# Stage 1 of a three-stage attention kernel: one hand-written issue sequence per pair of heads instead of a loop over tiles

## The chip, the cores and the metric

One core of one Trainium2 chip runs the whole program. The metric is the device time of one execution in microseconds (us): the median of several runs, set beside one execution that the hardware profiler recorded.

## What is computed

Three blocks run one after the other. Block 1, the one that the change touches, is attention whose queries are the means of two neighbouring positions, for 4 batches and 8 heads, with 576 queries, 1152 keys and head size 64:

```python
q_pool = q.reshape(B, H, S // 2, 2, D).mean(axis=3)
scores = scale * np.matmul(q_pool, k.transpose(0, 1, 3, 2))
scores = scores - np.max(scores, axis=-1, keepdims=True)
attn = np.exp(scores)
attn = attn / (np.sum(attn, axis=-1, keepdims=True) + 1e-09)
return np.matmul(attn, v).astype(np.float32)
```

Block 2 takes the result as 4 x 576 x 512 and runs causal attention with four experts, of which a gate picks two for each token. Block 3 multiplies a value projection by the sigmoid of a short causal convolution and projects the product.

## The kernel before

The program is scheduled by hand: each engine runs its instructions in the order in which the Python code issues them. It has three stages, one for each block. The change is in stage 1, lines 308 to 636.

**Tiles of stage 1.** The 8 heads of a batch go by twos, so there are 16 pairs (b, hp). The 576 queries of a head are four tiles of 128 rows and one of 64; the two rests of a pair share a tile. A pair thus has nine tiles, in two units (`UNITS`, line 390): unit 0 has the first two query tiles of both heads (tiles 0 to 3 of the pair), unit 1 the other two of both heads and the shared one (tiles 4 to 8). There are M = 144 tiles.

**What a tile goes through.** `scores` (line 394) multiplies a query tile by the keys, in three thirds g = 0, 1, 2 of 384 keys each. A third is two matmuls (L405), four for the shared tile; queries and keys are held as a high and a low part, which are added in PSUM. The tile's scores lie in three PSUM banks of pool `ps_s`, which has two such buffers. `rowmin` (L410, VectorE) takes the minimum of a row of all 1152 scores (they carry a minus sign). `expo` (L416, ScalarE) writes the exponentials to SBUF (tile `p`, three buffers) and their sums. `transp` (line 445) transposes a third on TensorE, three 128 x 128 transpositions (L453) into one bank of pool `ps_t`, which has two; one copy moves them from there into the unit's tile `pt`. For g = 0 and 1 the copy is on ScalarE (L461), for g = 2 on VectorE (L463).

**End of a unit.** `shares` (line 418) computes one over each row's sum on VectorE (L425, L426) and has GpSimd spread it (L431, L433). `av` (line 465) transposes these (L442, two or three matmuls; both banks used are of `ps_t`), has ScalarE copy them (L475, L479), and multiplies `pt` by the values, 18 pairs of matmuls (L483): the attention run. VectorE then multiplies by the shares (L485, tile `xf`), GpSimd splits the result, and a DMA writes it for stage 2. In the middle of `av`, `between` issues one `expo` and some steps of the preparation of later weights on VectorE (lines 92 to 105).

**What sets the order.** One loop over m (line 556) issues, in each turn, the transpositions of tile m - 2, the scores of tile m + 1, `expo(m)`, `shares(m - 1)` and pieces of other work: the queries and keys of the next pair on GpSimd (`prep`, L384, L361, L362, four pieces), which go to their place by DMA, the loads of the pair after that, and weight preparation. The thirds take turns in this order, in which 0 is a transposition and 1 a score group; after an attention run they alternate:

```python
for what, g in ((0, 0), (1, 0), (0, 1), (1, 1), (0, 2), (1, 2)) if burst else ((0, 0), (0, 1), (1, 0), (0, 2), (1, 1), (1, 2)):
```

Work that one turn produces for GpSimd or for DMA waits in the list `late` and is issued at the start of the next turn. After the last score tile, pieces of stage 2 (`fill`: projections L237 and L268) are issued between the transpositions.

Of the kernel before, what the change touches and what calls it, by code (L numbers as in the profile page):

```python
# [20 lines left out]
def tile_kernel(ctx, tc, q, k, v, w_gate, wq, wk, wv, wo, w_val, conv_w, w_out, wo_t, out):  # L21
    nc = tc.nc
    B, H, S, D = v.shape
# [20 lines left out]
                       fill=1.0, base=0, channel_multiplier=1)  # L44
# [8 lines left out]
                       fill=1e9, base=0, channel_multiplier=1)  # L53
# [162 lines left out]
    late2, urgent, rides = [], [], []  # L216
# [86 lines left out]

    G = 3
    GW = 3 * P

    s2 = ctx.enter_context(ExitStack())
    with ExitStack() as s1:
# [26 lines left out]
        pairs = [(b, hp) for b in range(B) for hp in range(H // 2)]  # L335
# [14 lines left out]
        def prep(n):  # L350
# [36 lines left out]

            return [lambda: one(0), qgroup, lambda: one(1), lambda: one(2)]

        UNITS = ([(0, 0), (0, 1), (1, 0), (1, 1)], [(0, 2), (0, 3), (1, 2), (1, 3), (2, 4)])  # L390
        tiles = [(n, u, i, ht) for n in range(len(pairs)) for u in range(2) for i, ht in enumerate(UNITS[u])]
        soft, pts, rss = {}, {}, {}
# [14 lines left out]
        def rowmin(m):  # L407
            d = soft[m]
            d["nm"] = st_p.tile([P, 1], F32, name="nm")
            dve.tensor_reduce(d["nm"], d["s"][:, :, 0:GW], axis=AX.XY, op=ALU.min)  # L410

        def expo(m):
            d = soft[m]
            n, u, i, _ = tiles[m]
            d["p"] = p_p.tile([P, G, GW], F32, name="p")
            act.activation(d["p"], d["s"][:, :, 0:GW], AF.Exp, bias=d["nm"], scale=-1.0, accum_out=sums[(2 * n + u) % len(sums)][:, i:i + 1])  # L416
# [28 lines left out]
        def transp(m, g):  # L445
            n, u, i, (h, t) = tiles[m]
            p = soft[m]["p"]
            if i == 0 and g == 0:
                pts[n, u] = pt_p.tile([P, C, 2, 256 + R64 * u], F32, name=f"pt{u}")
            pt = pts[n, u]  # L450
            ps = ps_t.tile([P, 512], F32, name="t")
            for j in range(3):
                pe.transpose(ps[:, j * P:(j + 1) * P], p[:, g, j * P:(j + 1) * P], ident)  # L453
            if h < 2:
                dst = pt[:, 3 * g:3 * g + 3, h, (t % 2) * P:(t % 2) * P + P]
                src = ps[:, 0:GW].rearrange("p (c k) -> p c k", k=P)
            else:
                dst = pt[:, 3 * g:3 * g + 3, :, 256:]
                src = ps[:, 0:GW].rearrange("p (c h k) -> p c h k", h=2, k=R64)
            if g < 2:  # L460
                act.activation(dst, src, AF.Copy)  # L461
            else:
                dve.tensor_copy(dst, src)  # L463
# [31 lines left out]
            late.append(high)  # L495

        Q0 = 2 * P
        PM = 1

        def first():  # L500

# [48 lines left out]
        load(1)  # L550
        nc.sync.dma_start(data[0][2], v[0, 0:2].rearrange("h (p c) d -> p h c d", p=P))
        bg, bgw = iter(()), iter(())
        LAG = 2
        M = len(tiles)
        burst, done = False, set()
        for m in range(-1, M + LAG + 4):
            if m == M - 9:
                assert not preps and next(bg, bg) is bg and next(bgw, bgw) is bgw
                s1a.close()
# [28 lines left out]
            now, late[:] = late[:], []  # L588
            for a in now:
                a()  # L590
            for what, g in ((0, 0), (1, 0), (0, 1), (1, 1), (0, 2), (1, 2)) if burst else ((0, 0), (0, 1), (1, 0), (0, 2), (1, 1), (1, 2)):
                if what == 0:
                    if 0 <= m - LAG < M:
                        transp(m - LAG, g)
                    if m >= M:
                        now2, late2[:] = late2[:], []
                        if fill:
                            fill.pop(0)[1]()
                        for a in now2:
                            a()  # L600
                        if urgent:
                            urgent.pop(0)()
                        if not fill and late2:
                            for a in late2:
                                a()
                            late2.clear()
                    if g == 1:
                        if m in (0, 1):
                            begin[m]()
                        if 0 <= m < M and m not in done:  # L610
                            expo(m)
                        if m in (2, 3):
                            begin[m]()
                    if g == 2:
                        if 0 <= m - 1 < M:
                            shares(m - 1)
                        if preps:
                            preps.pop(0)()
                elif 0 <= m + 1 < M:
                    scores(m + 1, g)  # L620
            if 0 <= m + 1 < M:
                rowmin(m + 1)
            burst = 0 <= m - LAG < M and tiles[m - LAG][2] == len(UNITS[tiles[m - LAG][1]]) - 1
            if burst:
                def between():
                    if m + 1 < M:
                        expo(m + 1)
                        done.add(m + 1)
                    for _ in range(9):
                        if next(bg, None):  # L630
                            break

                av(*tiles[m - LAG][0:2], between)
            next(bgw, None)
        for a in late:
            a()

# [452 lines left out]
```

## Time and profile before

| | |
|---|---|
| median of 3 runs | 794.48 us (794.35 to 795.16) |
| the profiled execution | 794.37 us |
| its span, first to last instruction | 792.6 us |
| mean granted clock of TensorE | 0.995 |
| busy in the span: TensorE, VectorE, ScalarE, GpSimd | 765.4, 541.9, 477.1, 304.7 us |
| transpositions of stage 1 (L453) | 1296, 278 ns of one |
| score matmuls (L405) | 960, about 370 ns of one |
| reductions (L410) | 144, 1348 ns of one |
| exponentials (L416) | 144, 1222 ns of one |
| copies on ScalarE (L461) | 288, 489 ns of one |
| copies on VectorE (L463) | 144, 558 ns of one |

How to read it. The span is what the profiler saw; the execution's own time is 1.8 us longer. The time of one instruction on TensorE runs from its start to a modelled end, and instructions overlap: the next starts before the one ahead has ended. So the sum of durations is more than the time that a sequence takes. Weight loads of TensorE have rows of their own (PEld). A share of busy time is a mean over three stages with different work; the rows below are therefore taken from stretches of stage 1, which ends with the last attention run.

### The profile page before, as it was taken

How to read it: one execution, taken by the hardware profiler on the slowest of the kernel's cores; microseconds unless marked ns; L12 is line 12 of the kernel's file. 1: busy time of each engine (PE TensorE's matmuls, PEld its weight loads, DVE VectorE, ACT ScalarE, POOL GpSimd, SP SyncE). 2: the span in 40 equal slices, each digit the busy share in tenths (PEclk: the TensorE clock that was granted, in tenths of full speed). 3: DMA queues.
4: the chain of work that ended last, by engine and by line, in shares of the span. 5: the costliest groups of instructions: out<-in, count | busy, mean ns of one | idle time of the engine just before them, and what ended most of it. 6: DMA issues, size and time to landing. Idle time of an engine off the chain costs nothing.

```text
span 792.6 us, 14790 instructions
## 1 busy us (share of the span) xinstructions
PE 765.4 (97%) x5332; PEld 625.5 (79%) x5332; DVE 541.9 (68%) x999; ACT 477.1 (60%) x1052; POOL 304.7 (38%) x412
## 2 busy tenths in 40 slices
PE   6899999999999999999999999997999999989998
PEld 4777877778778778778777787897988989877887
DVE  5666788778778878656655664355679898887730
ACT  5676677567667666766775675433464555648532
POOL 4454665664665665643433511021222222230000
PEclk9999999999999999999999999998999999999999
DMA  7777867868878688567458481455375454900112
GB/s 236 194 188 220 243 174 222 236 183 239 207 225 247 188 244 259 152 199 216 120 174 233 102 263 71 104 142 155 74 218 127 98 178 118 288 10 15 70 64 93
DMA packets 86248, 134.50 MB, mean 170 GB/s; under 512 B 21536, under 2 KB 58912, under 8 KB 86176
## 3 DMA queue, kind: packets, MB, share of 16 engines
q1 hardware_dynamic: 86176, 133.57, 59.6%
q8 instruction: 42, 0.69, 0.3%
q14 instruction: 30, 0.25, 0.1%
HBM read 53.37 MB, written 21.76 MB: 95 GB/s over the span
## 4 chain that ended last, share of the span: by engine, by line
PE 79%; DVE 10%; ACT 5%; DMA 2%; issue 2%; SPq 1%; POOLq 0%; ACTq 0%; DVEq 0%
PE s L405 19%; PE t L483 18%; PE t L453 15%; PE a L237 7%; PE o L1006 6%; PE a L268 4%; DVE nm L410 3%; ACT p L416 3%; PE a L798 3%; PE s L698 2%; PE a L663 2%; DVE gp L210 2%; DVE pt L463 1%; PE a L770 1%; PE t L442 1%
## 5 line engine op out<-in xcount | busy, mean ns | idle before, releaser
L410 DVE TENSOR_REDUCE nm<-s 128x1 f32<-128x1152 f32 x144 | 194.1, 1348 | 23.9 <-PE s L405 17.7
L461 ACT ACTIVATE pt<-t 128x384 f32<-128x384 f32 x288 | 132.6, 489 | 125.9 <-PE t L453 122.5
L453 PE MATMUL t<-ident,p 128*128 128x128 f32 x1296 | 204.8, 278 | 1.5 <-DVE pt L463 1.3
L416 ACT ACTIVATE p<-s,nm 128x1152 f32<-128x1152 f32 x144 | 176.0, 1222 | 36.8 <-DVE nm L410 34.1
L453 PEld LDWEIGHTS t<-ident,p 128*128 128x128 f32 x1296 | 150.9, 141 | 41.9 <-issue 13.5
L483 PE MATMUL t<-pt,vn 128*64 128x320 f32 (+1 forms) x1152 | 146.7, 408 | 0.1
L405 PE MATMUL s<-ka,qst 128*128 128x384 f32 x480 | 128.8, 372 | 8.6 <-ACT ka L535 6.8
L405 PE MATMUL s<-kb,qst 128*128 128x384 f32 x480 | 132.7, 369 | 1.4 <-ACT p L416 1.1
L483 PEld LDWEIGHTS t<-pt,vn 128*64 128x64 f32 x1152 | 80.0, 137 | 56.1 <-issue 5.0
L463 DVE COPY pt<-t 128x384 f32<-128x384 f32 x144 | 80.3, 558 | 63.9 <-PE t L453 59.3
L405 PEld LDWEIGHTS s<-ka,qst 128*128 128x128 f32 x480 | 77.9, 193 | 16.7 <-ACT p L416 8.9
L734 POOL TENSOR_TENSOR p<-p,sm 128x512 f32<-128x512 f32 (+3 forms) x32 | 40.1, 1253 | 114.3 <-DVE sm L732 85.9
L405 PEld LDWEIGHTS s<-kb,qst 128*128 128x128 f32 x480 | 77.6, 191 | 5.0 <-ACT p L416 1.7
L237 PE MATMUL a<-xh,wqk 128*128 128x288 f32 x384 | 59.6, 307 | 2.1 <-DVE pt L748 2.1
L485 DVE TENSOR_TENSOR xf<-t,rb 128x256 f32<-128x256 f32 (+1 forms) x32 | 14.7, 458 | 65.8 <-PE t L483 65.0
L237 PEld LDWEIGHTS a<-xh,wqk 128*128 128x128 f32 x384 | 54.7, 195 | 3.5 <-DVE pt L748 2.5
L431 POOL COPY rm<-rs 128x256 f32<-128x256 f32 x31 | 12.4, 398 | 92.2 <-PE t L453 58.5
L719 ACT ACTIVATE p<-s,nm 128x256 f32<-128x256 f32 (+3 forms) x64 | 33.0, 523 | 22.8 <-DVE nm L708 22.8
L362 POOL TENSOR_TENSOR hlk<-kt,hlk 128x384 fp32r<-128x384 f32 x45 | 45.5, 1010 | 1.1
L210 DVE SCALAR_TENSOR_TENSOR gp<-x,cw,gp 128x572 f32<-128x572 f32 (+3 forms) x48 | 41.0, 856 | 2.6 <-ACT gp L819 2.1
L492 POOL CAST xt<-xf 128x256 fp32r<-128x256 f32 (+1 forms) x32 | 13.6, 424 | 74.6 <-DVE xf L485 74.6
L708 DVE TENSOR_REDUCE nm<-s 128x2 f32<-128x512 f32 (+4 forms) x40 | 32.4, 811 | 1.4
(168 smaller groups left out, 1058.3 us busy)
## 6 DMA issues: line engine op xcount, KB each, us to landing
ka<-hlk SPq DMA_DIRECT2D x90, 192.0 KB, 3.2
kb<-hlk SPq DMA_DIRECT2D x90, 192.0 KB, 3.7
vn<-in_v_dram SPq DMA_DIRECT2D x16, 576.0 KB, 7.4
xh<-x_d SPq DMA_DIRECT2D x16, 576.0 KB, 6.5
k<-hl SPq DMA_DIRECT2D x32, 288.0 KB, 4.9
qt<-in_q_dram SPq DMA_DIRECT2D x15, 576.0 KB, 5.2
kt<-in_k_dram SPq DMA_DIRECT2D x15, 576.0 KB, 6.3
x_d<-xt SPq DMA_DIRECT2D x16, 320.0 KB, 4.0
```

The lines of the kernel that those rows point to most:

```text
L210: dve.scalar_tensor_tensor(out=gp[:, n:], in0=x[:, 0:SQ - n], scalar=cw[:, m, c:c + 1], in1=gp[:, n:], op0=ALU.mult, op1=ALU.add)
L237: pe.matmul(ps[:, 0:HQ], lhsT=wqk[wi][:, t, cs], rhs=xh[:, t, xi, qsl], start=o == 0, stop=o == len(ops) - 1)
L362: late.append(lambda: pool.tensor_tensor(out=hlk[:, 1, gs], in0=kt[:, gs], in1=f(hlk[:, 0, gs]), op=ALU.subtract))
L405: pe.matmul(ps[:, 0:GW], lhsT=a, rhs=c, start=o == 0, stop=o == len(ops) - 1)
L410: dve.tensor_reduce(d["nm"], d["s"][:, :, 0:GW], axis=AX.XY, op=ALU.min)
L416: act.activation(d["p"], d["s"][:, :, 0:GW], AF.Exp, bias=d["nm"], scale=-1.0, accum_out=sums[(2 * n + u) % len(sums)][:, i:i + 1])
L453: pe.transpose(ps[:, j * P:(j + 1) * P], p[:, g, j * P:(j + 1) * P], ident)
L461: act.activation(dst, src, AF.Copy)
L463: dve.tensor_copy(dst, src)
L483: pe.matmul(ps[64 * h:64 * h + 64, 0:N], lhsT=vn[:, h, j, :], rhs=pt[:, j, h, :], start=j == 0, stop=j == C - 1)
L734: pool.tensor_tensor(out=pv, in0=pv, in1=sm[:, :, None].to_broadcast([P, 2, w]), op=ALU.mult)
L1006: pe.matmul(ps[:, 0:w], lhsT=hl[xi][:, kt, t * P - a:(t + 1) * P - a], rhs=end3["wo3"][:, kt, wi, c:c + w], start=o == 0, stop=o == len(op ...
```

## The change

The loop over m is replaced by a string of 65 letters, issued once for each pair. T is one third of transpositions with its copy, S one score group, X an `expo`, H the `shares` of a unit, A the attention run of a unit (with an `expo` inside). Three tiles of scores are issued ahead. A second table, `EVAC`, says for each tile of a pair and each third whether its copy runs on ScalarE (A) or VectorE (D): 14 and 13 a pair, where it was 18 and 9. What a loop turn did besides (preparation, loads, the list `late`, the opening of stage 2's pools) is in `head(m)`, called ahead of the first score group of a tile; `filler` issues one piece of `fill`.

```diff
+        ORDER = "TSTSSTTXSTTSSHTTXSTTSSTTXSSSASTSSTXSTTSSTTXSTTSSHTTXSTTSSTTSTXSSA"
+        EVAC = ('DDA', 'ADD', 'AAD', 'DAA', 'DAD', 'DAA', 'DDA', 'ADD', 'AAA')
...
-            if g < 2:
+            if EVAC[m % 9][g] == "A":
                 act.activation(dst, src, AF.Copy)
             else:
                 dve.tensor_copy(dst, src)
...
-        for m in range(-1, M + LAG + 4):
+        def head(m):
...
+            if m >= M + 2:
+                for g in range(3):
+                    filler()
...
+        def score(k, g):
+            if g == 0:
+                head(k - 1)
+            if k < M:
+                scores(k, g)
+                if g == 2:
+                    rowmin(k)
+            if g == 2:
+                if preps:
+                    preps.pop(0)()
+                next(bgw, None)
+
+        def burst(m):
+            def between():
+                if m + 3 < M:
+                    expo(m + 3)
+                for _ in range(9):
+                    if next(bg, None):
+                        break
+
+            av(*tiles[m][0:2], between)
...
+        for n in range(len(pairs)):
+            for c in ORDER:
+                if c == "S":
+                    score(ns // 3, ns % 3)
+                    ns += 1
+                elif c == "T":
+                    transp(nt // 3, nt % 3)
+                    nt += 1
+                    if ns > 3 * M + 3:
+                        filler()
...
+                elif c == "X":
+                    if nx < M:
+                        expo(nx)
...
+                    nx += 1
+                elif c == "H":
+                    shares(9 * n + (3 if nt < 27 * n + 12 else 8))
+                elif c == "A":
+                    burst(nt // 3 - 1)
+                    nx += 1
```

The lines that follow show the order of instructions; in the changed kernel every line number of this part is higher by 4 (L405 is L409, L453 is L457, L463 is L467).

TensorE, unit 0 of a pair, from the attention run before it. `t<-ident,p` are transpositions, `s<-ka` and `s<-kb` scores of the two heads. Before:

```order
L483 MATMUL t<-pt_424,vn 64x320 x18
L453 MATMUL t<-ident,p 128x128 x3
L405 MATMUL s<-kb,qst_139 128x384 x2
L453 MATMUL t<-ident,p 128x128 x3
L405 MATMUL s<-kb,qst_139 128x384 x2
L453 MATMUL t<-ident,p 128x128 x3
L405 MATMUL s<-kb,qst_139 128x384 x2
L453 MATMUL t<-ident,p 128x128 x6
L405 MATMUL s<-ka,qst_138 128x384 x2
L453 MATMUL t<-ident,p 128x128 x3
L405 MATMUL s<-ka,qst_138 128x384 x4
L453 MATMUL t<-ident,p 128x128 x6
```

and with the change:

```order
L487 MATMUL t<-pt_427,vn 64x320 x18
L457 MATMUL t<-ident,p 128x128 x3
L409 MATMUL s<-kb,qst_139 128x384 x2
L457 MATMUL t<-ident,p 128x128 x3
L409 MATMUL s<-kb,qst_139 128x384 x4
L457 MATMUL t<-ident,p 128x128 x6
L409 MATMUL s<-ka,qst_138 128x384 x2
L457 MATMUL t<-ident,p 128x128 x6
L409 MATMUL s<-ka,qst_138 128x384 x4
L457 MATMUL t<-ident,p 128x128 x6
L409 MATMUL s<-ka,qst_138 128x384 x2
L457 MATMUL t<-ident,p 128x128 x6
```

Transpositions now come by sixes with two or four score matmuls between them; before, a three stood between the two score matmuls and the four.

VectorE in the same place. `xf` is the end of the attention run, `pt<-t` a copy, `nm<-s` a reduction, `rs` the shares. Before:

```order
L485 TENSOR_TENSOR xf_2560<-t,rb 128x320
L463 COPY pt_2618<-t 128x3x128
L410 TENSOR_REDUCE nm<-s 128x1
L463 COPY pt_2618<-t 128x3x128
L410 TENSOR_REDUCE nm<-s 128x1
L463 COPY pt_2618<-t 128x3x128
L425 TENSOR_SCALAR rs<-sums_142 128x4
L426 RECIPROCAL rs<-rs 128x4
L410 TENSOR_REDUCE nm<-s 128x1
```

and with the change:

```order
L489 TENSOR_TENSOR xf_2561<-t,rb 128x320
L467 COPY pt_2609<-t 128x3x128 x2
L414 TENSOR_REDUCE nm<-s 128x1
L467 COPY pt_2609<-t 128x3x128 x2
L414 TENSOR_REDUCE nm<-s 128x1
L429 TENSOR_SCALAR rs<-sums_142 128x4
L430 RECIPROCAL rs<-rs 128x4
L467 COPY pt_2609<-t 128x3x128 x2
L414 TENSOR_REDUCE nm<-s 128x1 x2
```

Copies come by twos ahead of each reduction, and the two small operations of the shares stand behind a reduction and ahead of two copies.

TensorE in the last pair, behind its last score group. The projections of stage 2 (`a<-xh`) follow. Before:

```order
L405 MATMUL s<-kb,qst_139 128x384 x2
L453 MATMUL t<-ident,p 128x128 x12
L237 MATMUL a<-xh,wqk_91 128x288
```

and with the change:

```order
L409 MATMUL s<-kb,qst_139 128x384 x2
L457 MATMUL t<-ident,p 128x128 x21
L237 MATMUL a<-xh,wqk_91 128x288
```

Seven thirds now stand in a row there instead of four.

## Rows read from the trace of the kernel before

**Rows 1.** Busy time by stretch: length, engines (instructions), granted clock, DMA share, GB/s.

```profile
core 0: us, PE busy (x) PEld busy (x) DVE busy (x) ACT busy (x) POOL busy (x), PEclk, DMA share, GB/s
...
160.00:220.00 60.00, 59.78 (x430) 46.33 (x428) 47.74 (x75) 39.96 (x79) 36.38 (x55) 1.00 0.77 213
...
498.00:501.00 3.00, 2.75 (x21) 2.41 (x20) 1.92 (x2) 2.01 (x5) 0.00 (x0) 1.00 0.00 0
...
542.50:549.50 7.00, 6.22 (x26) 5.86 (x26) 2.18 (x4) 1.52 (x6) 0.57 (x1) 0.52 0.33 129
```

**Rows 2.** Timeline, TensorE, unit 0 of a pair: start, length, engine, line, operation.

```profile
264.44 0.55 PE L453 MATMUL t<-ident,p 128*128 128x128 f32 x3
...
265.17 0.55 PE L453 MATMUL t<-ident,p 128*128 128x128 f32 x3
...
266.59 1.01 PE L453 MATMUL t<-ident,p 128*128 128x128 f32 x6
...
267.05 0.31 PEld L453 LDWEIGHTS t<-ident,p 128*128 128x128 f32 x3 [0.21 <-DVE pt L463]
...
267.35 0.60 PE L405 MATMUL s<-ka,qst 128*128 128x384 f32 x2
...
268.82 0.82 PE L453 MATMUL t<-ident,p 128*128 128x128 f32 x6
...
269.72 0.30 PEld L405 LDWEIGHTS s<-ka,qst 128*128 128x128 f32 x2 [0.32 <-ACT p L416]
...
273.37 0.38 PE L442 MATMUL t<-ident,rm 128*128 128x128 f32 x2
```

**Rows 3.** Timeline, TensorE, unit 1 of the same pair.

```profile
277.72 0.55 PE L453 MATMUL t<-ident,p 128*128 128x128 f32 x3
278.02 0.59 PE L405 MATMUL s<-kb,qst 128*128 128x384 f32 x2
278.45 0.49 PE L453 MATMUL t<-ident,p 128*128 128x128 f32 x3
278.69 0.59 PE L405 MATMUL s<-kb,qst 128*128 128x384 f32 x2
...
281.59 0.60 PE L405 MATMUL s<-ka,qst 128*128 128x384 f32 x2
...
283.07 0.82 PE L453 MATMUL t<-ident,p 128*128 128x128 f32 x6
283.64 0.59 PE L405 MATMUL s<-ka,qst 128*128 128x384 f32 x2
...
284.44 0.96 PE L405 MATMUL s<-ka,qst 128*128 128x384 f32 x4
...
289.74 0.49 PE L442 MATMUL t<-ident,rm 128*128 128x128 f32 x3
```

**Rows 4.** Timeline, VectorE (DVE) and ScalarE (ACT), unit 0 of that pair.

```profile
265.75 0.49 ACT L461 ACTIVATE pt<-t 128x384 f32<-128x384 f32 x1 [0.24 <-PE t L453]
...
266.44 0.56 DVE L463 COPY pt<-t 128x384 f32<-128x384 f32 x1 [1.32 <-PE t L453]
...
266.91 1.35 DVE L410 TENSOR_REDUCE nm<-s 128x1 f32<-128x1152 f32 x1
...
268.35 1.22 ACT L416 ACTIVATE p<-s,nm 128x1152 f32<-128x1152 f32 x1 [0.23 <-DVE nm L410]
...
269.02 1.36 DVE L410 TENSOR_REDUCE nm<-s 128x1 f32<-128x1152 f32 x1
...
269.57 0.86 ACT L461 ACTIVATE pt<-t 128x384 f32<-128x384 f32 x2
...
271.18 0.19 DVE L425 TENSOR_SCALAR rs<-sums 128x4 f32<-128x4 f32 x1
...
271.50 1.33 DVE L410 TENSOR_REDUCE nm<-s 128x1 f32<-128x1152 f32 x1
```

**Rows 5.** Timeline, TensorE, last pair: from its last score group to stage 2's first projection.

```profile
498.65 0.82 PE L453 MATMUL t<-ident,p 128*128 128x128 f32 x6
...
500.40 0.78 PE L237 MATMUL a<-xh,wqk 128*128 128x288 f32 x4
```

More of the change, by code (lines that the diff above doesn't have):

```diff
@@ L305, in tile_kernel @@
     GW = 3 * P
+    xh_p = y12_p = xh = wv3 = hl2 = c2 = qs = ks = v_p = g_p = ps_m = v2s = gws = None
+    fill = []
     s2 = ctx.enter_context(ExitStack())
@@ L497, in tile_kernel @@
         Q0 = 2 * P
-        PM = 1
         def first():
@@ L552, in tile_kernel @@
         bg, bgw = iter(()), iter(())
-        LAG = 2
         M = len(tiles)
-        burst, done = False, set()
-        for m in range(-1, M + LAG + 4):
+        def head(m):
+            nonlocal preps, bg, bgw
+            nonlocal xh_p, y12_p, xh, wv3, hl2, c2, qs, ks, v_p, g_p, ps_m, v2s, gws, fill
             if m == M - 9:
@@ L590, in tile_kernel @@
                 a()
[L591 to L634, printed above, removed]
+            if m >= M + 2:
+                for g in range(3):
+                    filler()
@@ new lines, in filler @@
+        def filler():
+            now2, late2[:] = late2[:], []
+            if fill:
+                fill.pop(0)[1]()
+            for a in now2:
+                a()
+            if urgent:
+                urgent.pop(0)()
+            if not fill and late2:
+                for a in late2:
+                    a()
+                late2.clear()
+        def score(k, g):
[9 more added lines that the diff above has]
+                next(bgw, None)
@@ new lines, in burst @@
+        def burst(m):
[6 more added lines that the diff above has]
+            av(*tiles[m][0:2], between)
+        ns, nt, nx = 0, 0, 0
+        for m in range(3):
+            if m:
+                head(m - 1)
+                begin[m - 1]()
+                expo(m - 1)
+            else:
+                head(-1)
+            for g in range(G):
+                scores(m, g)
+            rowmin(m)
+            if m and preps:
+                preps.pop(0)()
@@ new lines, in tile_kernel @@
+        ns, nx = 9, 2
+        for n in range(len(pairs)):
[8 more added lines that the diff above has]
+                        filler()
+                    if nt == 2:
+                        expo(2)
+                        begin[2]()
+                        nx = 3
+                elif c == "X":
+                    if nx < M:
+                        expo(nx)
+                    if nx == 3:
+                        begin[3]()
+                    nx += 1
[4 more added lines that the diff above has]
+                    nx += 1
@@ L635, in tile_kernel @@
+        for m in range(M + 2, M + 7):
+            head(m)
         for a in late:
```

## The prediction

> **What bounds the kernel now.** I began with the busy time by stretch [rows 1]. Inside stage 1 TensorE is busy 59.78 of 60 us at a granted clock of 1.00; VectorE has 47.74 us, ScalarE 39.96. So only TensorE's own stream can be shortened. But "busy" hides waits here, since the end of a matmul is modelled: what counts is when the next group starts. So I went on to the timeline of TensorE through the two units of one pair [rows 2, 3], read from the start of one row to the start of the next, and to the timeline of VectorE and ScalarE beside it [rows 4].
>
> Call three transpositions (one PSUM bank, one copy) a T, and the two score matmuls of one third of a tile an S; S3.1 is third 1 of tile 3. Where nothing waits, a T that is followed by an S takes 0.24 us (278.45 to 278.69), a run of two T 0.57 (283.07 to 283.64), one S 0.43 (278.02 to 278.45), eight score matmuls 1.48 (281.59 to 283.07) [rows 3]. So one more T costs 0.33, one more S (1.48 - 0.43) / 3 = 0.35, two S 0.78.
>
> Unit 0 lasts from 264.44 to 273.37, 8.93 us [rows 2]. Its 12 T and 12 S at the undisturbed prices (six single T, three double, six single S, three double) make 6 x 0.24 + 3 x 0.57 + 6 x 0.43 + 3 x 0.78 = 8.07, so 0.86 us are waits. Unit 1 lasts from 277.72 to 289.74, 12.02 us [rows 3]; seven single T, four double, six single S, four double and the 1.48 make 11.14: 0.88 us of waits. That is 1.74 us a pair, 28 us in 16 pairs: all that any new order of the same matmuls can win.
>
> Two waits make most of it. **The bank of a T.** There are two PSUM banks for transpositions, so a T waits for the copy of the T two before it. The double T at 266.59 took 0.76 instead of 0.57 for that reason: the bank came free when VectorE's copy (266.44, 0.56 us) ended, and the weight load followed 0.05 us later [rows 2, 4]. **The score tile.** Scores have two buffers, so the first S of tile k+2 waits for the exponential of tile k: from the last S of a tile (ends 268.82) 0.20 us until the reduction starts (269.02) [rows 2, 4]; the reduction is 1.35, then 0.09 (266.91 to 268.35), the exponential 1.22, and 0.15 until the weight load at 269.72, which the profile puts down to it [rows 2, 4]. Sum: 0.20 + 1.44 + 1.22 + 0.15 = 3.01 us. Between these two points the old order has TT S T SS TT, 0.57 + 0.43 + 0.24 + 0.78 + 0.57 = 2.59: 0.42 us short, and the double T at 268.82 shows most of it, 0.90 instead of 0.57 [rows 2]. A restarted T loses 0.06 more (after the attention run the T at 277.72 takes 0.30, not 0.24 [rows 3]), so 0.05 + 0.06 = 0.11 lie between the end of a copy and an undisturbed stream.
>
> **The change, part by part.**
>
> *Order of TensorE.* Nothing is added or taken away; in mid-unit a tile becomes TT S TT SS. Between the last S of tile k and the first of k+2 there is now TT S TT SS TT, 0.57 + 0.43 + 0.57 + 0.78 + 0.57 = 2.92 us, plus the bank wait worked out next, 0.18: 3.10 against 3.01. The score wait goes, with 0.09 us to spare. What is late next is the bank. In TT S TT the third T comes 2 x 0.33 + 0.35 = 1.01 after the first, but its bank needs 0.53 (a T's start to its copy: 265.17 to 265.75 less the 0.06 of a restart) + 0.49 (that copy; two in a row take 0.86) + 0.11 = 1.13 [rows 2, 4]: a wait of 0.12. The old order shows just this where a double T starts undisturbed: the S and T that follow it last from 283.64 to 284.44, 0.80 instead of 0.43 + 0.24 [rows 3]. The fourth T needs the second copy on the same engine: 0.53 + 0.86 + 0.11 = 1.50 against 1.13 + 0.33 = 1.46, 0.05 more. So one such passage costs 0.18, and each unit has two of them (both with the first pair of copies on ScalarE): 0.36.
>
> *The rest of unit 0.* TensorE's restart after the long run of attention times V, 0.06 (the rows of the T at 264.44 and at 265.17 show 0.55, not 0.49), and as much for the second T, which waits for the bank of that run; both as now [rows 2]. The two small divisions (H in the table of letters) now sit ahead of two copies on VectorE: 0.32 us (271.18 to 271.50 [rows 4]), which makes T3.2 about 0.05 late. Sum 0.53 against 0.86: 0.33 won.
>
> *Unit 1.* It now begins with scores instead of a T. No row shows that entry; I keep the 0.06, between 0 and 0.15. Two passages 0.36; T8.1 behind copies that the divisions delayed, 0.05; T8.2 one S after T8.1, its bank at 1.13 against 0.33 + 0.33 + 0.05 + 0.35, 0.07. Sum 0.54 against 0.88: 0.34 won.
>
> *Copies.* Four a pair move from ScalarE to VectorE (13 and 14 instead of 9 and 18). In the fullest stretch a pair of 30.7 us holds 47.74 / 60 x 30.7 = 24.4 us of VectorE; 4 x 0.56 = 2.2 more make 26.7 of 30.0, 89%. On the path this costs nothing as long as a tile's round on VectorE is shorter than TensorE's 4 x 0.33 + 3 x 0.35 = 2.37 (2.55 with its bank wait). By the rows, where the next instruction starts 0.47 after a copy's start (266.44 to 266.91) [rows 4], the round is 0.47 + 0.47 + 1.35 = 2.29: it fits, and with the divisions, 2.61, it is late once by the 0.05 counted above. Without that overlap it would not fit (second rival).
>
> *What else moves.* The spreading of the shares stands before the next pair's query addition on GpSimd, not behind; its two copies have over 2 us before the attention run needs them, so nothing is gained or lost. The issues on SyncE keep their order but for two weight loads that trade places with a neighbour; no row of stage 1 has TensorE waiting for them. The key transfers keep their distance of five tiles.
>
> *The ends.* The first 27 us wait for loads and the start; I give pair 0 the same gain as the others (bounds 0 and 1 us). In the last pair no scores are left, and seven T stand in a row instead of four: four took 1.75 us (498.65 to 500.40) instead of 1.30 [rows 5], 0.45 of waits; seven make about 0.85, so 0.4 lost. Five filler groups instead of six are issued before the last attention run; the work is the same. The last unit 1 wins nothing.
>
> **Sum.** 16 x 0.33 + 15 x 0.34 - 0.4 = 10.0 us, on the profiled 794.37: 784.4, and as the median of the runs (794.48) is the same within 0.02%, I forecast **784.4 us**. Bounds: passages without the second term and without the late T (0.13 each) give 0.38 and 0.32 a unit, 16 us won, 778; passages with the two copies not overlapped (0.13 + 0.16) and 0.16 at every late T give 0.86 and 0.96, nothing won, 796. The forecast's own range is 780 to 790.
>
> **The rivals.** A difference under 0.2% (1.6 us) can't be told from none here.
>
> 1. *No change: the bank takes all that the score tile gives.* That is the upper bound above, 793 to 796. For it: the copies of a passage now share one engine. Against it: the two in 0.86 us [rows 4]. Chance 0.14.
>
> 2. *Slower: VectorE becomes the bound of mid-unit.* If adjacent copies do not overlap, a round costs 2 x 0.56 + 1.35 + three gaps of about 0.1 = 2.77, over 2.55 by 0.22. From there it decides: each round pushes the reduction, the exponential and the bank back. With five such rounds a pair (the others lie behind an attention run, in which VectorE catches up) it is 1.1 us on top of 1.07: 2.17 against 1.74, 0.43 x 16 = 7 us slower, 801. For it: VectorE is the fullest engine after TensorE and no row shows two copies in a row there. Against it: the 0.47 us. Chance 0.11.
>
> 3. *More than forecast: nearly every wait goes* because copies start earlier than the rows say; 0.3 us left a pair, 23 us won, 771. Against it: the 0.13 that the old order shows. Chance 0.06.
>
> 4. *The clock drops in the row of seven T.* In the old run the granted clock fell once, to 0.52 over 542.50 to 549.50 [rows 1], nearly all of it at the lower level of 1.2 GHz; 7 us at that level cost 3.4 us. A second such fall would give 788. Chance 0.03, for four T in a row ran at 1.00 (498 to 501 [rows 1]). The Trainium skill ("TensorE: Matmul & The Clock Gate", Part 4, PE-mode transpose) says that transpositions do not count as work for the clock gate, which would make longer rows of them a risk; the 1.00 does not bear it out for twelve transpositions in a row, and a run of six is all that mid-unit has.
>
> **How the numbers follow.** Forecast 0.66, rivals 0.14, 0.11, 0.06, 0.03. Of the first rival 0.02 falls below 792.8 and 0.01 above 796.0. Faster: 0.66 + 0.06 + 0.03 + 0.02 = 0.77; same 0.11; slower 0.12. The range leaves out the second rival, most of the third and a little of the first: 779 to 793.
>
> **What would show it.** Right: a pair about 0.65 us shorter; the double T without waits inside and instead 0.12 us between S and the next double T; no weight load of scores in stage 1 that waits for the exponential; VectorE near 89% in its fullest stretch, with adjacent copies 0.47 apart; the row of 21 transpositions near 3.1 us. Wrong: score loads that still wait for the exponential (the 3.01 was too short), T that wait for VectorE by more than 0.1 (rival 2), or a clock under 1.00 in stage 1.

## The result, and the profile after

The changed kernel takes **787.62 us** (median of 5 runs, 787.25 to 789.49) against 794.52 us for the kernel before (median of 5, 794.35 to 795.32): a ratio of 0.9919, 95% interval 0.9905 to 0.9932, so 6.9 us faster. Forecast were 784.4 us, 10.1 under that median, and a range of 779 to 793. The sign and the cause hold; the size is two thirds.

The profiled execution of the changed kernel is the slowest of its five (789.49 us, span 787.7), so the accounting here goes by the point where stage 2's first score group starts: 521.23 us in the old trace, 515.08 in the new one, 6.15 us earlier. Behind that point the program is the same, and its length differs from run to run (last section).

Busy time by stretch, changed kernel (columns as in [rows 1]); the first row is the stretch of [rows 1], the second the start of the program:

```profile
160.00:220.00 60.00, 59.83 (x432) 47.03 (x430) 53.17 (x84) 37.07 (x72) 37.98 (x55) 1.00 0.77 214
...
20.00:24.00 4.00, 2.40 (x18) 1.83 (x16) 3.94 (x6) 1.82 (x5) 3.71 (x4) 1.00 0.36 90
```

VectorE has 53.17 of 60 us, 89%, as forecast, and TensorE's busy time is as full as before. Here too it says nothing of where the time went, so on to TensorE's timeline: unit 0 of one pair, and unit 1 of another, read from start to start as [rows 2, 3].

```profile
50.05 0.55 PE L457 MATMUL t<-ident,p 128*128 128x128 f32 x3
...
51.86 0.82 PE L457 MATMUL t<-ident,p 128*128 128x128 f32 x6
52.44 0.59 PE L409 MATMUL s<-ka,qst 128*128 128x384 f32 x2
52.94 0.93 PE L457 MATMUL t<-ident,p 128*128 128x128 f32 x6
53.62 0.96 PE L409 MATMUL s<-ka,qst 128*128 128x384 f32 x4
...
56.95 0.82 PE L457 MATMUL t<-ident,p 128*128 128x128 f32 x6
57.53 1.30 PE L409 MATMUL s<-kb,qst 128*128 128x384 f32 x6
58.67 0.38 PE L446 MATMUL t<-ident,rm 128*128 128x128 f32 x2
...
274.96 0.62 PE L409 MATMUL s<-kb,qst 128*128 128x384 f32 x2
275.41 0.49 PE L457 MATMUL t<-ident,p 128*128 128x128 f32 x3
...
280.08 0.59 PE L409 MATMUL s<-ka,qst 128*128 128x384 f32 x2
280.58 0.93 PE L457 MATMUL t<-ident,p 128*128 128x128 f32 x6
...
285.18 0.60 PE L409 MATMUL s<-kb,qst 128*128 128x384 f32 x2
285.67 0.55 PE L457 MATMUL t<-ident,p 128*128 128x128 f32 x3
285.97 0.94 PE L409 MATMUL s<-kb,qst 128*128 128x384 f32 x4
286.75 0.49 PE L446 MATMUL t<-ident,rm 128*128 128x128 f32 x3
```

Unit 0 lasts from 50.05 to 58.67, 8.62 us instead of 8.93 [rows 2]; unit 1 from 274.96 to 286.75, 11.79 instead of 12.02 [rows 3]. The double T takes 0.58 (51.86 to 52.44) where it took 0.76 and 0.90, and the wait now stands behind it: S 0.50 instead of 0.43 (52.44 to 52.94) and the next double T 0.68 instead of 0.57 (52.94 to 53.62). That is 0.07 + 0.11 = 0.18 us a passage, the forecast figure, and it recurs at 280.08. VectorE, ScalarE and the weight loads beside that unit:

```profile
52.39 0.87 ACT L465 ACTIVATE pt<-t 128x384 f32<-128x384 f32 x2 [4.64 <-PE t L457]
52.93 0.69 PEld L457 LDWEIGHTS t<-ident,p 128*128 128x128 f32 x6 [0.22 <-ACT pt L465]
...
53.52 1.02 DVE L467 COPY pt<-t 128x384 f32<-128x384 f32 x2
54.61 1.36 DVE L414 TENSOR_REDUCE nm<-s 128x1 f32<-128x1152 f32 x1
```

Two copies on VectorE take 1.02 us, so the second starts some 0.47 after the first, and the reduction (54.61) starts 0.07 after both have ended: the round fits. The chain is where the sum put it: copy on ScalarE, then the weight load of the second double T at 52.93, put down to it. The waits of TensorE's weight loads from 45 to 460 us (total us, times, longest), after:

```profile
PEld t L457 <- ACT pt L465: 14.6, 66, 0.2
...
PEld t L457 <- DVE pt L467: 0.4, 2, 0.2
PEld s L409 <- ACT p L420: 0.2, 1, 0.2
```

and before:

```profile
PEld s L405 <- ACT p L416: 8.4, 28, 0.4
PEld t L453 <- DVE pt L463: 5.7, 27, 0.2
PEld t L453 <- ACT pt L461: 3.3, 16, 0.2
```

The score tile's wait is gone (8.4 to 0.2 us), and the bank on ScalarE's copies has taken its place (3.3 to 14.6, never over 0.2 at once). The totals include idle time beside matmuls that were still streaming, so they name the waits; the prices are those of the timeline.

Where the 6.15 us lie, from the starts of the share transpositions (R, L446; L442 before) of unit 0 and unit 1 of the first pair (pair 0), of unit 1 of the last pair but one, and from stage 2's first scores:

| stretch | before, us | after, us | gained | forecast |
|---|---|---|---|---|
| start to R of pair 0, unit 0 | 27.32 | 28.47 | -1.15 | |
| start to R of pair 0, unit 1 | 43.77 | 44.63 | -0.86 | 0.67 |
| 14 further pairs | 430.76 | 423.28 | 7.48 | 9.38 |
| last pair | 46.70 | 47.17 | -0.47 | -0.07 |
| sum, to stage 2's first scores | 521.23 | 515.08 | 6.15 | 10.0 |

So 0.53 us a pair against 0.67, pair 0 loses where it was to gain, and the last pair loses more than forecast. In the units shown above unit 0 gives 0.31 and unit 1 0.23; the mean of the 14 pairs is 0.26 for each. Unit 0 is longer in four pairs of the changed kernel (counted from 0, pairs 4, 5, 6 and 8: 8.70, 8.67, 8.95 and 8.85 us), and one unit 1 of the kernel before took 12.33.

### The profile page after: what moved, and what is told of

It is laid out like the page before. It is cut to its first block, busy times and chain, and to the rows that moved or that the text cites. A ratio compares the mean times of both kernels' runs of the same rounds, so it can differ in the third digit from the quotient of the medians.

```text
span 787.7 us, 14786 instructions
## 1 busy us (share of the span) xinstructions
PE 760.3 (97%) x5332; PEld 624.9 (79%) x5332; DVE 574.5 (73%) x1063; ACT 448.2 (57%) x988; POOL 306.4 (39%) x412
## 4 chain that ended last, share of the span: by engine, by line
PE 86%; DVE 5%; DMA 4%; ACT 2%; issue 1%; SPq 1%; POOLq 0%; DVEq 0%; ACTq 0%
PE s L409 21%; PE t L457 20%; PE t L487 18%; PE a L237 6%; PE o L1046 6%; PE a L268 4%; PE a L838 3%; DMA xh<-x_d 2%; PE s L738 2%; PE a L703 2%; PE a L810 1%; DMA k<-hl 1%; PE t L446 1%; PE s L745 1%; DVE gp L210 1%
## 5 line engine op out<-in xcount | busy, mean ns | idle before, releaser
L457 PE MATMUL t<-ident,p 128*128 128x128 f32 x1296 | 194.6, 281 | 3.2 <-DVE pt L467 2.6
L465 ACT ACTIVATE pt<-t 128x384 f32<-128x384 f32 x224 | 100.0, 489 | 147.2 <-PE t L457 137.6
L457 PEld LDWEIGHTS t<-ident,p 128*128 128x128 f32 x1296 | 147.4, 141 | 42.2 <-ACT pt L465 17.4
L409 PE MATMUL s<-ka,qst 128*128 128x384 f32 x480 | 128.2, 370 | 6.8 <-ACT ka L538 6.8
L409 PE MATMUL s<-kb,qst 128*128 128x384 f32 x480 | 120.8, 360 | 1.6 <-ACT p L420 1.0
L467 DVE COPY pt<-t 128x384 f32<-128x384 f32 x208 | 107.4, 548 | 13.2 <-PE t L457 10.0
L409 PEld LDWEIGHTS s<-kb,qst 128*128 128x128 f32 x480 | 79.6, 191 | 8.7 <-issue 6.2
L409 PEld LDWEIGHTS s<-ka,qst 128*128 128x128 f32 x480 | 78.0, 193 | 8.5 <-ACT ka L538 7.2
```

What stands on the lines that cost most here:

```text
L409: pe.matmul(ps[:, 0:GW], lhsT=a, rhs=c, start=o == 0, stop=o == len(ops) - 1)
```

## The experiments

Times of one execution are read at the rows of the table above, since the rest of the program adds a spread of its own; "pair" is the time from one pair's R to the next in mid-stage, "u0" and "u1" the two units there.

| kernel | R pair 0, u0 | R pair 0, u1 | pair | u0 / u1 | last pair | stage 2's scores | whole, us |
|---|---|---|---|---|---|---|---|
| before | 27.32 | 43.77 | 30.72 | 8.93 / 12.03 | 46.70 | 521.23 | 794.52 (median of 5) |
| changed | 28.47 | 44.63 | 30.20 | 8.62 / 11.79 | 47.17 | 515.08 | 787.62 (median of 5) |
| old_copies | 25.56 | 43.25 | 32.93 | 9.82 / 13.35 | | | 826.02 |
| new_copies | 27.78 | 47.79 | 33.6 | 9.15 / 13.15 | | | 841.87 |
| short_before | 23.45 | 43.78 | 30.33 | 8.70 / 11.86 | | | 788.80 |
| short_after | 24.32 | 41.92 | 30.16 | 8.60 / 11.79 | | | 784.52 |
| start | 28.32 | 44.45 | 30.15 | 8.62 / 11.78 | 47.21 | 514.50 | 788.27 |
| entry | 28.29 | 44.40 | 30.13 | 8.62 / 11.75 | 47.13 | 514.08 | 788.40 |
| tail | 28.48 | 44.60 | 30.15 | 8.62 / 11.78 | 46.68 | 514.26 | 786.36 |
| all_three | 28.13 | 44.23 | 30.14 | 8.62 / 11.75 | 46.67 | 513.56 | 786.89 (median of 5) |
| start4 | 25.76 | 42.01 | | | 47.17 | 512.29 | 785.06 |
| warm | 28.44 | 44.57 | | | 47.16 | 514.64 | 785.53 |
| best | 27.74 | 43.94 | | | 46.66 | 513.24 | 787.04 (median of 4) |
| best_warm | 27.75 | 43.95 | | | 46.66 | 513.22 | 786.35 (median of 6) |

**The two halves of the change apart.** old_copies has the new order with the old rule for copies, new_copies the old order with the new table.

```diff
-        EVAC = ('DDA', 'ADD', 'AAD', 'DAA', 'DAD', 'DAA', 'DDA', 'ADD', 'AAA')
+        EVAC = ('AAD',) * 9
```

> The new order with the old choice of engines (thirds 0 and 1 of every tile copied on ScalarE, third 2 on VectorE). My theory: order and copies belong together. The copy of T0.2 on VectorE now stands behind the reduction of tile 3, which starts before it and holds VectorE 1.3 us, so T1.1 waits about 1.1 us for its bank; the like happens in the other passages where a reduction or an exponential is ahead of a copy. About three such waits a pair: a pair of 33 us or more instead of 30.2, 830 us in all (over 805 for certain). Rival: the order alone brings the gain and the engine of a copy is indifferent; then 787 to 790 us.

```diff
+        EVAC = ('DDA', 'ADD', 'AAD', 'DAA', 'DAD', 'DAA', 'DDA', 'ADD', 'AAA')
...
-            if g < 2:
+            if EVAC[m % 9][g] == "A":
```

> The old order with the new choice of engines. My theory: in five of nine tiles the first third is now copied on VectorE, right behind the reduction of another tile, which holds the copy back by about 1.3 us and the third third with it: 3 to 5 us more a pair, 840 to 870 us. Rival: what helped was that ScalarE was relieved of four copies a pair; then this alone would be faster than 794 us, towards 788.

Each half alone loses: 826.02 us with the new order, 841.87 with the new copies, a pair of 32.93 and 33.6 us, as both theories had it. Weight loads that waited, 45 to 460 us, in the kernel with the new order and the old copies:

```profile
PEld t L457 <- ACT pt L465: 31.3, 84, 0.5
...
PEld t L457 <- DVE pt L467: 20.0, 50, 0.7
```

and in the one with the old order and the new copies:

```profile
PEld t L484 <- ACT pt L462: 24.0, 25, 1.1
...
PEld t L454 <- DVE pt L464: 17.2, 24, 1.2
```

In old_copies T waits for copies 134 times (84 and 50), up to 0.7 us instead of 0.2; the theory had fewer and longer waits, three of about 1.1 us a pair. The score tile's wait is not in the list, which goes down to 0.3 us; since the longer waits for copies also give the exponential more time, this run alone doesn't show that the order took it away. The table of copies is what keeps the bank from costing more than the score tile did. In new_copies the last copies of a unit come late, and the attention run (L484 there) waits for them, 25 times and up to 1.1 us. So the rival, that ScalarE's relief alone brings the gain, falls.

**The reduction cut to half.** If the score tile's chain is what held the old order, a shorter reduction frees the old order and leaves the new one alone. short_before and short_after have the same edit:

```diff
-            dve.tensor_reduce(d["nm"], d["s"][:, :, 0:GW], axis=AX.XY, op=ALU.min)
+            dve.tensor_reduce(d["nm"], d["s"][:, :, 0:GW // 2], axis=AX.XY, op=ALU.min)
```

> The kernel before, with the reduction of a tile over half of the scores (the first 192 of each third), which shortens the chain from scores to exponential by about 0.6 us and changes nothing on TensorE. My theory: the wait for the score tile is what the old order lost most by; with a chain of 2.4 instead of 3.0 us the 2.59 us between two uses of a score buffer are enough, so unit 0 goes from 8.93 to about 8.65 and unit 1 from 12.02 to about 11.75; a pair 0.5 to 0.6 us shorter, 785 to 787 us in all. Rival: the waits are for banks alone; then the pair stays at 30.7 us and the time within 2 us of 794.

> The changed kernel with the same short reduction. My theory: its pair no longer waits for the score tile but for banks in four passages of 0.18 us, which the reduction does not touch; only the thirds that are late on VectorE gain, 0.05 each: a pair of 30.1 instead of 30.2 us, and pair 0 some tenths shorter; 785 to 787 us. Rival: VectorE's load is what holds the changed kernel (each of its rounds is fuller by two copies); then the pair falls by 0.3 us or more, under 29.9, and the total to 783 or less.

The old order's pair fell from 30.72 to 30.33, by 0.39 (0.5 to 0.6 forecast); the new one's from 30.20 to 30.16, by 0.04. As a whole short_before missed its 785 to 787 us (788.80), and short_after came in just under its own (784.52). In short_after unit 0 of pairs 4, 5, 6 and 8 took 8.60 to 8.61 like the others, so what lengthens them in the changed kernel is VectorE. TensorE's timeline of short_before shows why 0.39:

```profile
267.39 0.82 PE L453 MATMUL t<-ident,p 128*128 128x128 f32 x6
...
267.96 0.59 PE L405 MATMUL s<-ka,qst 128*128 128x384 f32 x2
...
268.46 0.55 PE L453 MATMUL t<-ident,p 128*128 128x128 f32 x3
...
268.76 0.96 PE L405 MATMUL s<-ka,qst 128*128 128x384 f32 x4
```

The double T at 267.39 is undisturbed, 0.57, and its weight loads no longer wait for an exponential. But S and T behind it take 0.50 and 0.30 instead of 0.43 and 0.24: 0.13 of bank wait, the figure of [rows 3] that the sum was built on. Whoever frees the score tile meets the bank next, in either order.

**Three losses that the first reading named**, one edit each. start has the old copies in the first tile of the stage; entry puts a T ahead of unit 1's scores; tail moves one S of the last pair's second unit ahead of two T. That S has no scores left to do, but it counts: from there on a filler group (projections of stage 2) follows every T, so the fillers begin two T earlier and the row is five T long.

```diff
-            if EVAC[m % 9][g] == "A":
+            if (EVAC[m % 9][g] if m else "AAD"[g]) == "A":
```

> The changed kernel, but the first tile of all copies its thirds 0 and 1 on ScalarE and 2 on VectorE, as before the change. My theory: the changed kernel loses 1.15 us in unit 0 of pair 0 (R at 28.47 instead of 27.32 us) since those first copies stand on VectorE behind the reduction of tile 2 and ahead of the splitting of the queries, which delays the reduction of tile 3 from 18.5 to 19.9 us. With them on ScalarE that comes back: R of pair 0 at 27.2 to 27.6, the rest unchanged; 1 us less in all. Rival: the loss comes from the loads and the splitting on GpSimd; then R stays at 28.3 to 28.6.

```diff
-        ORDER = "TSTSSTTXSTTSSHTTXSTTSSTTXSSSASTSSTXSTTSSTTXSTTSSHTTXSTTSSTTSTXSSA"
+        ORDER = "TSTSSTTXSTTSSHTTXSTTSSTTXSSSATSSSTXSTTSSTTXSTTSSHTTXSTTSSTTSTXSSA"
```

> The changed kernel, with one transposition third between the attention run of unit 0 and the scores of tile 7 (ATSSST in place of ASTSST in the table of letters). My theory: unit 1 won 0.20 instead of 0.34 us because scores pay for starting behind an attention run (0.11 us against 0.06) and because the string there changes kind twice more often. A pair 0.05 to 0.1 us shorter, 1 us in all. Rival: the entry is indifferent, and the missing 0.14 lies in the last passages of the unit; then the pair stays at 30.20.

```diff
+        LAST = ORDER[0:46] + ORDER[46:].replace("HTTXS", "HSTTX")
...
-            for c in ORDER:
+            for c in ORDER if n < len(pairs) - 1 else LAST:
```

> The changed kernel; in the last pair alone the letter that opens stage 2's pools comes two thirds earlier, so that five instead of seven thirds of transpositions stand in a row without other work, and two more pieces of stage 2 are issued before the last attention run. My theory: the row of seven takes 3.70 us instead of 2.28 for want of banks, and the two that get projections between them no longer wait: 0.5 us less until the first scores of stage 2. Rival: the first projection waits for a score buffer that the exponential of the last tile still holds; then nothing is won or some tenths lost.

> The three edits of the runs above together (first tile's copies, entry of unit 1, last pair). If each does what my theory says, the sum is 2 to 2.5 us under the changed kernel's 787.6: 785.3 us, in the profile a pair of 30.1 us, R of pair 0 at 27.4. If only one holds, 786.6 us or more.

start missed: 28.32 against 28.47, so the first tile alone is not it; 28.32 also lies in the band of its rival, the loads and the splitting on GpSimd. entry won 0.03 to 0.05 us of unit 1 (11.75, against 11.78 to 11.79 in the kernels with the old entry), tail 0.49 us of the last pair (46.68). TensorE's timeline of the row in the changed kernel:

```profile
490.86 0.82 PE L457 MATMUL t<-ident,p 128*128 128x128 f32 x6
491.93 0.93 PE L457 MATMUL t<-ident,p 128*128 128x128 f32 x6 [0.25 <-ACT pt L465]
493.13 1.68 PE L457 MATMUL t<-ident,p 128*128 128x128 f32 x9 [0.27 <-DVE pt L467]
494.56 1.85 PE L237 MATMUL a<-xh,wqk 128*128 128x288 f32 x12
```

and in tail:

```profile
492.78 0.55 PE L458 MATMUL t<-ident,p 128*128 128x128 f32 x3 [0.27 <-DVE pt L468]
493.09 1.85 PE L237 MATMUL a<-xh,wqk 128*128 128x288 f32 x12
```

The row of 21 takes 3.70 us (490.86 to 494.56): 1.07 for the first two T, 1.20 for the next two, 1.43 for the last three. tail's row of 15 starts at 490.51 and takes 2.58; what follows goes by single T between projections, 0.25 each, without a wait (494.77 to 495.02). All three edits together reach stage 2's scores at 513.56, 1.5 us before the changed kernel, but R of pair 0 came at 28.13, not at 27.4; the whole came out at 786.89 us instead of 785.3, ratio to before 0.9912 (0.9898 to 0.9925), which can't be told from the change's own 0.9919 (0.9905 to 0.9932).

**Pair 0.** Two theories were left: VectorE holds up the whole of unit 0 (start4: old copies in its first four tiles), or TensorE's clock, which in the changed kernel fell to 0.5 from 15.3 to 18.7 us (warm: four transpositions that nobody reads behind each of the first nine score groups).

```diff
-            if EVAC[m % 9][g] == "A":
+            if (EVAC[m % 9][g] if m > 3 else "AAD"[g]) == "A":
```

> The changed kernel, but all four tiles of unit 0 of pair 0 copy thirds 0 and 1 on ScalarE and 2 on VectorE. My theory: what pair 0 lost is a matter of VectorE in that whole unit, which also splits the first queries and keys, not of the first tile alone; the run with the old copies everywhere had R of pair 0 at 25.56 us, against 28.47. So R of pair 0 comes to 25.5 to 26.2 us if the granted clock is up by 15 us, to 26.3 to 27.3 if it rises at 17 to 19 us; 1.5 to 2.5 us less in all. Rival: it was the clock alone (full from 12.23 us in that run, from 18.74 in the changed kernel); then R stays at 28 or more whenever the clock rises at 17 us or later.

```diff
+        dummy = ps_t.tile([P, 512], F32, name="t")
+
+        def warm(n):
+            for _ in range(n):
+                pe.transpose(dummy[:, 0:P], ident, ident)
...
+                warm(4)
```

> The changed kernel with four transpositions of the identity that nobody reads behind each of the first nine score groups, to give TensorE something to do while it waits for loads. If a lower granted clock is part of what pair 0 lost (0.50 between 15.33 and 18.74 us in the changed kernel's profile, against 1.00 from 17.07 on before), the clock now is 1.00 from 12 us at the latest and R of pair 0 falls by 0.5 to 1.0 us, to 27.5 to 28.0. Rival: pair 0 follows VectorE's chain whatever the clock; then R stays within 0.2 us of 28.47, or is later by what the dummies cost.

warm brought the clock to 1.00 from 10.2 us on, and R stood at 28.44: the clock was not it. start4 put R at 25.76, 2.7 us earlier; that is the band that its theory gave for a clock that is up by 15 us, and here it was at 1.00 from 16.4, between the two cases of the theory. The last two kernels join start4, entry and tail, without and with warm's transpositions:

> The entry of unit 1, the last pair's letters and the copies of unit 0 of pair 0 changed together, as in the runs above. By the single runs: 14 pairs by 0.06 are 0.9 us, the last pair 0.5, pair 0 1.5 to 2.5: 3 to 4 us under 787.6, 784 us. If the copies of pair 0 do nothing, 786 us, as in the run of the three edits.

> The same with the dummy transpositions at the start. If the clock matters there, 0.5 to 1 us under the run before it, 783 to 783.5 us, and a smaller spread from run to run; if not, the same or some tenths slower.

Here R came at 27.74 and 27.75, with the clock up from 16.8 and from 9.6 us, though unit 0 had the same copies as in start4. Up to R, old_copies, start4 and best issue the same instructions in the same order on every engine, so the 2 us between 25.56 and 25.76 on one side and 27.74 on the other lie in how long the same operations took, not in what was issued. VectorE of start4 (the last line is the spreading of the shares, which in this one unit is VectorE's):

```profile
19.66 0.93 DVE L534 SCALAR_TENSOR_TENSOR qst<-pt,qst 64x256 fp32r<-64x256 f32 x2
...
22.47 0.17 DVE L429 TENSOR_SCALAR rs<-sums 128x4 f32<-128x4 f32 x1
...
22.89 0.58 DVE L435 COPY rm<-rs 128x256 f32<-128x256 f32 x1
```

VectorE, GpSimd and TensorE of best (each line number of theirs is one higher):

```profile
19.76 1.64 DVE L535 SCALAR_TENSOR_TENSOR qst<-pt,qst 64x256 fp32r<-64x256 f32 x2
...
22.05 0.87 PE L458 MATMUL t<-ident,p 128*128 128x128 f32 x6 [1.02 <-DVE pt L468]
...
23.29 0.53 DVE L430 TENSOR_SCALAR rs<-sums 128x4 f32<-128x4 f32 x1
...
23.88 1.42 POOL L381 TENSOR_TENSOR hlq<-qp,hlq 128x576 fp32r<-128x576 f32 x1
24.07 1.38 DVE L436 COPY rm<-rs 128x256 f32<-128x256 f32 x1
...
25.97 0.87 PE L458 MATMUL t<-ident,p 128*128 128x128 f32 x6 [1.16 <-DVE pt L468]
```

The same three operations took 0.93, 0.17 and 0.58 us in start4 and 1.64, 0.53 and 1.38 in best, and TensorE waited 1.02 and 1.16 us for the copies that stand behind them. In start4 the first of these waits was 0.31 and the second did not occur: 0.71 + 1.16 = 1.87 of the 1.98 us between the two. Why these operations are long in one kernel and short in the other is argued in the last section, not shown by a run of its own.

As a whole, best took 787.04 us (ratio 0.9911, 0.9898 to 0.9923) and best_warm 786.35 (0.9905, 0.9889 to 0.9921), short of the 784 and the 783 to 783.5 that were expected. They reach stage 2's scores 1.84 and 1.86 us earlier than the changed kernel; neither can be told from it over the whole, so no version here is shown to be faster than the changed kernel.

## Why the prediction was right in sign, and the gain a third smaller

**What bounds the kernel: right.** The old stream lost its time to the score tile and the bank. The score tile's wait went when order and copies changed (8.4 to 0.2 us), and the halved reduction took it away in the old order too.

**Unit 0: right in most pairs.** 0.31 us won in the unit shown, 0.33 forecast. The passage costs 0.18, twice a unit (by the sum's own terms 0.17: 0.58 less 0.06 is 0.52, not 0.53, and 1.50 less 1.46 is 0.04). The T after the attention run and the T behind it lose 0.06 each, as counted. The late T (T3.2) came out at 0.01 us instead of 0.05. By the prediction's prices the new string of this unit is 8.09 us long (two single T, five double, three single S, three double, one triple at 1.13), not 8.07, and that is the missing 0.02.

What the sum left out is the rest of VectorE's work, which delays unit 0 in four of the 14 pairs: in pair 6 the multiplication that ends the attention run stands behind a step of weight preparation (L102, 200.79, 0.91 us) and the second T waits for its bank; in pair 8 the first small operation of the shares takes 0.41 us instead of 0.16 (267.60). The kernel before has unit 0 at 8.91 to 8.96 us in all 14.

**Unit 1: mechanism right, the size off.** The step that failed is "Sum 0.54 against 0.88: 0.34 won". It compared waits, as if the undisturbed price stayed 11.14. But the new string does not run at 11.14: the same matmuls fall into ten score groups and nine runs of T, and each change between the two kinds has its price. Priced with the prediction's own ledger (three single T, six double, four single S, five double, the 1.48) it is 0.72 + 3.42 + 1.72 + 3.90 + 1.48 = 11.24. The waits themselves measured 0.55 (11.79 less 11.24) against the 0.54 of the sum. So 0.10 of the missing 0.11 is book-keeping, 1.4 us in 14 pairs. That the waits agree to 0.01 is partly luck: the entry by scores, which no row had shown, cost 0.02 (0.45 from 274.96 to 275.41, less 0.43) and not 0.06, T8.1 next to nothing and not 0.05, and the S and T of T8.2 0.12 (0.49 and 0.30, 285.18 to 285.97) and not 0.07; the rest are hundredths in other groups.

**Pair 0: wrong.** The step is "The first 27 us wait for loads and the start; I give pair 0 the same gain as the others (bounds 0 and 1 us)". It lost 0.86 us, outside its bounds. The rows that would have told it were there to be read. Busy time by stretch, and TensorE's two long waits in that unit, kernel before:

```profile
20.00:24.00 4.00, 2.71 (x19) 2.38 (x18) 3.91 (x5) 2.58 (x5) 3.76 (x4) 1.00 0.29 72
...
22.25 0.55 PE L453 MATMUL t<-ident,p 128*128 128x128 f32 x3 [1.29 <-DVE pt L463]
...
27.32 0.41 PE L442 MATMUL t<-ident,rm 128*128 128x128 f32 x2 [0.69 <-DVE rm L431]
```

and the same waits in the changed kernel:

```profile
22.94 1.01 PE L457 MATMUL t<-ident,p 128*128 128x128 f32 x6 [1.60 <-DVE pt L467]
...
26.56 1.01 PE L457 MATMUL t<-ident,p 128*128 128x128 f32 x6 [0.77 <-DVE pt L467]
```

VectorE has 3.91 of 4.00 us there and TensorE only 2.71: in pair 0 VectorE also splits the first queries (L531; L534 after), and GpSimd is nearly as full. In this one unit TensorE waited for VectorE already, and the change gave VectorE two more copies in the first four tiles (six instead of four). Two copies take it 1.02 us; R of unit 0 moved by 1.15. VectorE as the bound is what the second rival feared for mid-unit, but not by its condition: copies overlap here too, and it is the splitting that fills the engine. Two experiments show that VectorE is the place. With the reduction cut to half R came 3.9 us earlier in the old kernel (23.45) and 4.1 in the new one (24.32). And without the two extra copies it came at 25.56 to 27.75 in all four executions (old_copies, start4, best, best_warm), against 28.13 to 28.48 in the six that have the full reduction and five or six of the copies on VectorE. But the copies are not all of it: with four of them R stood at 27.32 in the old kernel and at 27.74 in best, where VectorE's small operations lasted longer. So the two copies cost pair 0 between 0.7 and 2.7 us, and how much of it is their own length and how much those operations stays open.

**The last pair: mechanism right, the size off.** The step is "seven make about 0.85, so 0.4 lost". It roughly doubled the 0.45 of four T in a row [rows 5], which was small already: by the prediction's own prices four T take 0.24 + 3 x 0.33 = 1.23 us, not 1.30. In a row without scores the third, the fifth and the seventh T wait, three times and not twice. Less 0.33 for each T, and 0.24 for the last, the three parts of the row hold 0.41 (1.07 until 491.93), 0.54 (1.20 until 493.13) and 0.53 us of waits (1.43 until 494.56): 1.48 instead of 0.85, and 3.70 us instead of 3.1. The pair lost 0.47 instead of 0.07, 0.40 more than forecast, and tail gave 0.49 back; where the other 0.2 us of those waits were made good was not traced.

**The rivals.** No change, and nearly all waits gone, did not come. A slower mid-unit from VectorE did not come: adjacent copies overlap as they did on ScalarE, and weight loads of T waited for VectorE's copies 0.4 us in all. The clock did not fall in the row of seven T: the granted clock from 484 to 496 us was 1.00, with 21 transpositions in a row. The Trainium skill ("TensorE: Matmul & The Clock Gate", Part 4, PE-mode transpose) would have had them not count as work; the trace again doesn't bear it out. The chances left one slip: the range of 779 to 793 ends where the first rival's 793 to 796 begins, so it leaves out nearly all of that rival, not a little of it.

**The sum.** Of the 3.83 us missing at stage 2's scores (9.98 less 6.15), the 14 pairs make 1.90, pair 0 1.53 and the last pair 0.40. Of the 1.90, unit 1 makes 1.15 and unit 0 0.94, most of it in the four longer units; the attention runs, for which nothing was forecast, gained 0.19.

## What to carry to other kernels

When an order is rewritten, price the whole new string with the same ledger before you compare waits: a term that "stays" hides there. A free buffer gives its place to the next one in line, so work out that one's chain too, and move the engine that empties it along with the order. And give the first and the last pass rows of their own: an engine that is not the bound in the middle (47.74 of 60 us) can be the bound at the start (3.91 of 4.00), and the change is paid there.

## What the runs showed of the hardware

**Small operations on VectorE that last as long as GpSimd's.** The addition of a constant to 128x4 numbers, the first operation of the shares, took 0.16 to 0.17 us in at least 28 of the 32 units of every kernel (start4, 22.47) but, in unit 0 of pair 0, 1.41 in the kernel before and 0.82 in the changed one. VectorE and GpSimd, kernel before:

```profile
24.08 1.41 POOL L379 TENSOR_TENSOR hlq<-qp,hlq 128x576 fp32r<-128x576 f32 x1
24.11 1.41 DVE L425 TENSOR_SCALAR rs<-sums 128x4 f32<-128x4 f32 x1
```

and changed:

```profile
24.02 1.42 POOL L381 TENSOR_TENSOR hlq<-qp,hlq 128x576 fp32r<-128x576 f32 x1
...
24.64 0.82 DVE L429 TENSOR_SCALAR rs<-sums 128x4 f32<-128x4 f32 x1
```

Both VectorE operations end 0.02 to 0.03 us after the GpSimd operation that had started ahead of them (25.52 and 25.49, 25.46 and 25.44), and best's 128x256 copy ends 0.15 after it (25.45 and 25.30). The Trainium skill ("SBUF — State Buffer", Who interferes with whom) says that the two engines share a pair of ports that one of them holds for a whole instruction while the other blocks, for some forms of VectorE's operations. These ends agree with that; against it stands start4's 0.17 us at 22.47, beside a GpSimd scaling that ran from 21.68 to 23.33. The splitting (L534) fits too: it ended 0.08 us after a GpSimd operation in both kernels, in start4 after the shorter one (20.59 and 20.51) and in best after the next, longer one (21.40 and 21.32). Which forms block was not tried by itself, so for best against start4 this stays the likeliest reading: there a few tenths of a microsecond would decide which of VectorE's operations meets which of GpSimd's.

**A fall of the clock in stage 2 that has two lengths.** In each of the kernels named here the granted clock falls to 0.50, the lower level of 1.2 GHz, once between 530 and 550 us; in the kernel before TensorE was busy 4.29 of the 7.70 us ahead of it (535 to 542.7). It lasted some 6.8 us in the kernels before and changed, start, entry, all_three, start4 and best_warm (3.4 us lost), and 3.4 us in tail, warm and best (1.7 lost). From stage 2's first scores to the end of the span the first group needs 271.0 to 272.6 us, the second 269.0 to 270.3, in code that is the same. The two lengths account for 1.7 us of a spread of 3.6, which hides gains of 1 to 2 us in stage 1.

**The clock at the start is as uneven.** The traces record it from its rise on; in start4, where it rose at 16.4 us, the T at 15.39 took 0.50 us and the one at 16.56 0.24. The time from which it stayed at 1.00 lay between 9.6 and 19.9 us in twelve of the fourteen kernels; in new_copies and short_before it fell once more, from 29.7 to 33.1 and from 43.6 to 47.0, behind stretches in which TensorE was busy 1.14 of 2.60 and 1.60 of 3.60 us. And R of pair 0 did not follow it: 28.32 us in start (from 19.9) and 28.44 in warm (from 10.2).
